# Packed attention with a feed-forward layer: where the third and fourth quarter of a batch's packs are computed

## The chip, the cores and the metric

The kernel runs on one core of a Trainium2 chip. The metric is the time of one execution on the device in microseconds. TensorE (PE in the profile) multiplies matrices, VectorE (DVE) and ScalarE (ACT) work on elements, GpSimd (POOL) adds a few weights early on, and SyncE (SP) issues the DMAs.

## The reference

For each of 8 batches and 8 heads, 32 packed queries `p` attend to 576 keys and values; the result serves as both keys and values for the 576 queries `q`. The heads are then laid side by side into 512 features, and a feed-forward layer without biases follows.

```python
def sm_attn(qq, kk, vv):
    s = scale * np.matmul(qq, kk.transpose(0, 1, 3, 2))
    s = s - np.max(s, axis=-1, keepdims=True)
    a = np.exp(s)
    a = a / (np.sum(a, axis=-1, keepdims=True) + 1e-09)
    return np.matmul(a, vv)
p_packed = sm_attn(p, k, v)                # 8 x 8 x 32 x 64
out = sm_attn(q, p_packed, p_packed)       # 8 x 8 x 576 x 64
...
x = out.transpose(0, 2, 1, 3).reshape(B * S, H * D)   # 4608 x 512
h = x @ w_in                               # 512 -> 2048
g = h * (1.0 / (1.0 + np.exp(-h)))
return g @ w_out                           # 2048 -> 512
```

All of it is float32. To keep its precision in the large products, each operand is split into an upper part (`hi`) that TensorE takes at its faster rate and the rest (`lo`), and three products hi·hi, hi·lo and lo·hi are added.

## The kernel before

**Packs.** The kernel does not form the attention's output `x`. The second attention's values are the 32 packed rows of each head, so `x @ w_in` is the attention's weights times (packed rows times the head's rows of `w_in`). This second factor is called the packs here. A batch's packs have 2048 columns and are made in four quarters of 512 (numbered 0 to 3), each by one `Packs` object: `products` (line 510) runs 16 matmuls of the 64x32 tiling through `heads` (line 250) into one buffer of the PSUM pool `ps_two`; `upper` (line 528) copies them to `pw_hi` on ScalarE; `lower` (line 531) subtracts on VectorE and gives `pw_lo`, after which the PSUM buffer is free.

**Units.** A batch's feed-forward layer is cut into 16 units, f = 0 to 15, of 128 hidden features each. A unit has a hidden block (`h_products`, line 563: 12 matmuls of 288 columns from one quarter of the packs and the second attention's weights; then `h_values`, lines 582 to 586, on ScalarE, and `h_lower`, line 593, on VectorE) and an output block (`out_products`, line 603: 12 matmuls of 512 columns). Unit f takes the quarter f // 4. The 64 tokens of a batch that don't fill a whole block of 128 are kept in `rest` and handled for two batches together, in four units of their own after every odd batch.

**Order.** The early part (batches 0 and 1, and the first steps of batch 2) follows an order written out by hand in `ORDER`. From line 761 on a loop runs over the units of batches 2 to 7. TensorE, VectorE, ScalarE and SP each execute their instructions in the order in which the program issues them; nothing is rescheduled on these four. `hidden_up_to(u + 2)` issues hidden blocks ahead, so that a unit's output block finds its values ready.

**The next batch's attention in between.** Beside the units of batch b the loop issues the attention of batch b + 1, one step at a given f (`STEPS_AT`):

- f=1, `scores1`: packed queries times keys in two halves of 288 keys, 16 matmuls each (line 250), each half into its own `ps_two` buffer; line 276 copies the first half out on ScalarE and the second on VectorE. Then the load of q and the maximum (lines 286 and 287, VectorE).
- f=2, `exps1`: exponentials on ScalarE (line 296) and the reciprocals of their sums on VectorE (lines 300 and 301).
- f=3, `turned1`: two transposes of 32x32 blocks on VectorE (line 309); then 16 small DMAs from SP (line 327), one for each pair of heads and each 32 partitions, lay the transposed blocks out over the partitions. Pair 0 is issued first, pair 3 last.
- f=7, `packed`: 80 small matmuls of these weights with v (line 348) into a `ps_two` buffer. They run over all four pairs for each chunk of keys. `scaled1` (line 358, VectorE) divides by the sums; after the unit's output block `turned` (line 367, TensorE) and `packs` (line 371, VectorE) transpose the result.
- f=9 to 12: the second attention's scores, exponentials and weights.

**PSUM.** `ps_two` has two buffers, given out in turn. Hidden blocks, quarters of packs, scores and products with v all take one each. Where a unit needs both (`all_banks`, line 772), no hidden blocks are issued ahead in it, and the next unit issues two.

**The quarters' places.** Quarters 0 and 1 of batch b + 1 are made at f = `PACKS_NEXT` = 13 of batch b. Quarters 2 and 3 are made at f = `PACKS_OWN` = 4 of the batch itself: both products, 32 matmuls in one block, then both splits. Batch 2 makes its quarters 1 and 2 earlier (line 767) and only quarter 3 at f=4. `pw_hi` and `pw_lo` have three buffers: two in `pw` and one in `pw_b`.

Of the kernel before, what the change touches and what calls it, by code (L numbers as in the profile page):

```python
# [20 lines left out]
B, H, S, D = 8, 8, 576, 64  # L21
# [9 lines left out]
FJ = JW // P  # L31
# [6 lines left out]
EARLY = 2  # L38
# [40 lines left out]
ON_POOL = (0, 1, 2, 6, 9, 10, 11, 13, 14, 15, 16, 18, 19)  # L79
ON_TOKENS = (0,)  # L80
PACKS_NEXT, PACKS_OWN = 13, 4
SCALE = 1.0 / math.sqrt(D)
EPS = 1e-9

# [4 lines left out]
def packed_attention_ffn(ctx: ExitStack, tc: tile.TileContext, pkT, qT, v, w_in, w_out, out):  # L89
# [56 lines left out]
    def load_k(b):  # L146
        t = kvq.tile([P, 5 * DM], F32, name="kvq_t")
        n = P + NI * HS
        for c in (slice(0, n), slice(n, n + NI * HS)) if b == 0 else (slice(0, P + NI * S),):
            nc.sync.dma_start(t[:, c], pkT[b, :, c])  # L150
        made["k", b] = t[:, :P], t[:, P : P + NI * S].rearrange("p (hf i s) -> p hf i s", hf=2, i=NI)

    def load_q(b):
        if b == 0:
            n = NI * MAIN
            spare = osb.tile([P, 2, DM], F32, name="o").rearrange("p r e -> p (r e)")
            parts_of_q = spare[:, :n], rest.rearrange("p f e h s -> p (f e h s)")[:, : NI * S - n]
            for t, c in zip(parts_of_q, (slice(0, n), slice(n, NI * S))):
                nc.sync.dma_start(t, qT[b, :, c])
            made["q", b] = [t.rearrange("p (i s) -> p i s", i=NI) for t in parts_of_q]  # L160
            return
        t = kvq.tile([P, 5 * DM], F32, name="kvq_t")
        nc.sync.dma_start(t[:, : NI * S], qT[b])
        t = t[:, : NI * S].rearrange("p (hf i s) -> p hf i s", hf=2, i=NI)
        made["q", b] = [t[:, 0], t[:, 1]]

    def load_v(b):
        t = kvq.tile([P, 5 * DM], F32, name="kvq_t")
        nc.sync.dma_start(t, v[b])
        made["v", b] = t.rearrange("p (c e) -> p c e", c=5)  # L170
# [84 lines left out]
    class Attention:  # L255
# [24 lines left out]
        def largest1(self, par=None):  # L280
# [5 lines left out]
            nc.vector.tensor_reduce(self.mx[:, c], s, axis=AX.X if self.b else AX.XY, op=ALU.max, negate=True)  # L286
            nc.vector.tensor_scalar(self.nm[:, c], self.mx[:, c], SCALE, None, op0=ALU.mult)

        def exps1(self, par):
# [5 lines left out]
            e = self.e1[:, par] if self.b else self.e1[:, par].rearrange("p (h s) -> p h s", h=2)  # L295
            nc.scalar.activation(e, s, AF.Exp, bias=self.nm[:, c], scale=SCALE, accum_out=self.den[:, c])  # L296

# [149 lines left out]
        def exps2(self, hf):  # L447
            if self.b in ON_TOKENS:
                _, t = self.on_tokens(hf)
                nc.scalar.activation(t, t, AF.Exp, scale=SCALE)  # L450
                return
            s2, e2 = self.half[hf]
            nc.scalar.activation(e2, s2, AF.Exp, scale=SCALE)

# [159 lines left out]
    def out_products(u, hf=None):  # L614
        b, f, *more = units[u]
        start = first_of(u)
        first = u == start
        if more:
            if first:
                acc[start, 0] = sum_banks()  # L620
            for n in range(FJ):
                products(acc[start, 0][:, 0], u, f + n, n, f + n == 0, f + n == NF - 1)
            return
        for h in range(2)[half_or_all(hf)]:
            if first:
                acc[start, h] = sum_banks()
            for k in range(2):
                products(acc[start, h][:, k], u, f, 2 * h + k, first, is_last(u))

    def out_rows(u, h):  # L630

        b, f, *more = units[u]
        sums = acc[first_of(u), h]
        if more:
            o = osb.tile([P, 2, DM], F32, name="o")
            nc.scalar.copy(o[:, 0], sums[:, 0])
            for n, (e, h) in enumerate((e, h) for e in range(2) for h in range(2)):
                at = (b + e) * S + h * HS + MAIN
                rows = slice((2 * e + h) * REST, (2 * e + h) * REST + REST)
                (nc.scalar if n % 2 and b == B - 2 else nc.sync).dma_start(out[at : at + REST], o[rows, 0])  # L640
            return
        if ("o", b, h) in outs:
            o = outs.pop(("o", b, h))
            nc.vector.tensor_tensor(o, sums, o, ALU.add)
        else:
            o = osb.tile([P, 2, DM], F32, name="o")
            (nc.vector.tensor_copy if h else nc.scalar.copy)(o, sums)
        if f == NF - 1:
            at = b * S + h * HS
            nc.sync.dma_start(out[at : at + MAIN].rearrange("(k p) e -> p k e", p=P), o)  # L650
        else:
            nc.sync.dma_start(parts[b, h], o)
# [53 lines left out]
    def hidden_up_to(u):  # L706
        nonlocal done
        while done < min(u, len(units) - 1):
            done += 1
            if len(units[done]) == 2:  # L710
                h_products(done)
            h_values(done)
            h_lower(done)

    def packs_in(b, *quarters):
        both = [Packs(b, FJ * j, FJ) for j in quarters]
        for part in both:
            part.products()
        for part in both:
            part.upper()  # L720
            part.lower()

    def step_of(b, step):
        at = attention[b]
        if step == "scores1":
            for hf in range(2):
                at.scores1(hf)
                at.copied1(hf)
            load_q(b)
            at.largest1()  # L730
        elif step == "exps1":
            for par in range(2):
                at.exps1(par)
            at.shares1()
        elif step == "turned1":
            for par in range(2):
                at.turned1(par)
            at.spread1()
        elif step == "packed":
            at.packed()  # L740
            at.scaled1()
            if b < B - 1:
                load_k(b + 1)
        elif step == "scores2":
            for hf in range(2):
                at.scores2(hf)
            for hf in range(2):
                at.turned2(hf)
            if b < B - 1:
                load_v(b + 1)  # L750
            for hf in range(2):
                at.less2(hf)
        else:
            for hf in range(2):
                if step == "split2":
                    at.upper2(hf)
                    at.lower2(hf)
                else:
                    getattr(at, step)(hf)

    for u in range(n_early, len(units)):
        b, f, *more = units[u]
        if more:
            hidden_up_to(u + 1 if u == n_early else u + 2)
            out_products(u)
            if u == n_early:
                packs_in(2, 1, 2)
            if f + FJ == NF:
                out_rows(u, 0)
            continue  # L770
        step = STEPS_AT.get(f) if b + 1 < B else None
        all_banks = step in ("scores1", "scores2") or f == PACKS_OWN or f == PACKS_NEXT and b + 1 < B
        if not all_banks:
            hidden_up_to(u + 2)
        if f == PACKS_OWN:
            packs_in(b, *((3,) if b == 2 else (2, 3)))
        if f == PACKS_NEXT and b + 1 < B:
            packs_in(b + 1, 0, 1)
        if step:
            step_of(b + 1, step)  # L780
        out_products(u)
        if f == NF - 1:
            for h in range(2):
                out_rows(u, h)
        if step == "packed":
            attention[b + 1].turned()
            attention[b + 1].packs()
# [43 lines left out]
```

## Time and profile before

| | us |
|---|---|
| Median of 3 runs | 703.89 (703.79 to 703.93) |
| The profiled execution | 703.09 |
| its span from first to last instruction | 701.3 |
| output products (line 603), three groups of 560 matmuls | 223.8 + 219.4 + 218.8 busy |
| hidden products (line 563), three groups | 154.6 + 146.5 + 145.9 busy |
| packs (line 250, from `win`), 560 matmuls | 32.8 busy |

Matmuls are pipelined, so the busy times of two groups overlap and their sum is larger than the span. The chain that ended last gives each moment to one instruction; the lengths of its pieces are used below. In its rows the columns are the start in the span, the length, the engine, the tile and line, and the number of instructions; in the timeline they are the start, the length, the engine, the line, the operation, the tiles with their shapes and the count, and in brackets how long the engine was idle before and what released it. SPq is SP's queue: its time is that of issuing a DMA, while the landing is given separately. By lines, the chain's time is distributed thus:

| line | what | share of the chain |
|---|---|---|
| 603 | output products | 58% |
| 563 | hidden products | 29% |
| 250 | packs and both attentions' scores | 7% |
| 348 | products with v | 2% |

### The profile page before, as it was taken

What the parts mean: (1) busy time and instruction counts of PE and PEld (TensorE: products, weight loads), DVE (VectorE), ACT (ScalarE), POOL (GpSimd) and SP (SyncE); (2) the same over time, 40 slices, a digit from 0 to 9 for tenths busy, and PEclk for the clock granted to TensorE, in tenths of its full rate; (3) what the DMA queues carried; (4) which work ended last, traced back from release to release, by engine and by line L of the source; (5) the groups of instructions that cost most, each with busy time, mean ns of one, the idle gap of its engine ahead of it and who ended that gap; (6) DMA issues with size and microseconds to landing.
All of it is one profiled execution on the core that took longest, in us unless ns stands there. A gap on an engine that the chain in (4) does not pass through costs nothing.

```text
span 701.3 us, 12059 instructions
## 1 busy us (share of the span) xinstructions
PE 693.3 (99%) x5058; PEld 560.5 (80%) x5058; DVE 326.2 (47%) x482; ACT 331.0 (47%) x614; POOL 28.7 (4%) x19
## 2 busy tenths in 40 slices
PE   8999999999999999999999999999999999999997
PEld 5557788878787888888788888878878788788886
DVE  4999948764534136333532335342372323622111
ACT  4997866637245244451633526452442533433221
POOL 1041022110000000000000000000000000000000
PEclk9999999999999999999999999999999999999999
DMA  9775333634221320313012131123202120010002
GB/s 358 288 304 206 134 121 114 193 141 156 70 81 69 77 104 1 128 33 137 12 61 84 27 107 49 61 72 70 110 0 76 68 36 1 1 60 1 1 1 75
DMA packets 28309, 64.61 MB, mean 92 GB/s; under 512 B 16736, under 2 KB 16736, under 8 KB 23904
## 3 DMA queue, kind: packets, MB, share of 16 engines
q1 hardware_dynamic: 28160, 63.71, 26.2%
q8 instruction: 40, 0.66, 0.4%
q10 hardware_dynamic: 96, 0.13, 0.1%
q14 instruction: 13, 0.11, 0.0%
HBM read 48.76 MB, written 11.53 MB: 86 GB/s over the span
## 4 chain that ended last, share of the span: by engine, by line
PE 97%; ACT 1%; DMA 1%; DVE 1%; issue 0%; ACTq 0%; DVEq 0%
PE ps_acc L603 58%; PE ps_two L563 29%; PE ps_two L250 7%; PE ps_two L348 2%; DMA kvq_t<-in_pkT 1%; PE ps_acc L250 0%; ACT tm L296 0%; PE ps_two L144 0%; ACT tm L392 0%; ACT w_raw L201 0%; ACT win L201 0%; PE ps_two L315 0%; PE ps_two L367 0%; PE ps_acc L315 0%; DVE mx L286 0%
## 5 line engine op out<-in xcount | busy, mean ns | idle before, releaser
L603 PE MATMUL ps_acc<-wo_hi,g_hi 128*128 128x512 f32 x560 | 223.8, 400 | 0.0
L603 PE MATMUL ps_acc<-wo_hi,g_lo 128*128 128x512 f32 x560 | 219.4, 392 | 0.0
L603 PE MATMUL ps_acc<-wo_lo,g_hi 128*128 128x512 f32 x560 | 218.8, 391 | 0.0
L593 DVE TENSOR_TENSOR g_lo<-g,g_hi 128x512 fp32r<-128x512 f32 x124 | 88.9, 717 | 259.5 <-ACT g_hi L584 259.5
L582 ACT ACTIVATE g<-ps_two 128x512 f32<-128x512 f32 x124 | 74.1, 598 | 263.9 <-PE ps_two L563 239.9
L563 PE MATMUL ps_two<-a_lo,pw_hi 128*128 128x288 f32 (+2 forms) x528 | 154.6, 301 | 0.1
L563 PE MATMUL ps_two<-a_hi,pw_hi 128*128 128x288 f32 (+1 forms) x496 | 146.5, 295 | 0.0
L563 PE MATMUL ps_two<-a_hi,pw_lo 128*128 128x288 f32 (+1 forms) x496 | 145.9, 294 | 0.0
L603 PEld LDWEIGHTS ps_acc<-wo_hi,g_hi 128*128 128x128 f32 x560 | 105.1, 188 | 39.3 <-issue 19.9
L603 PEld LDWEIGHTS ps_acc<-wo_hi,g_lo 128*128 128x128 f32 x560 | 105.1, 188 | 24.5 <-DVE g_lo L593 0.4
L603 PEld LDWEIGHTS ps_acc<-wo_lo,g_hi 128*128 128x128 f32 x560 | 105.2, 188 | 18.4
L563 PEld LDWEIGHTS ps_two<-a_lo,pw_hi 128*128 128x128 f32 x528 | 99.1, 188 | 6.2 <-issue 1.4
L563 PEld LDWEIGHTS ps_two<-a_hi,pw_hi 128*128 128x128 f32 x496 | 93.1, 188 | 4.5 <-issue 0.8
L563 PEld LDWEIGHTS ps_two<-a_hi,pw_lo 128*128 128x128 f32 x496 | 93.2, 188 | 0.0
L584 ACT ACTIVATE g_hi<-ps_two 128x512 fp32r<-128x512 f32 x124 | 73.6, 593 | 10.9 <-PE ps_acc L603 10.9
L531 DVE TENSOR_TENSOR pw_lo<-ps_two,pw_hi 128x1024 fp32r<-128x1024 f32 x31 | 36.8, 1219 | 12.8 <-ACT pw_hi L528 12.8
L528 ACT CAST pw_hi<-ps_two 128x1024 fp32r<-128x1024 f32 x31 | 30.2, 1015 | 20.9 <-PE ps_two L250 20.9
L250 PE MATMUL ps_two<-win,ppT 64*32 64x512 f32 (+1 forms) x560 | 32.8, 560 | 0.4 <-POOL win L220 0.4
L586 ACT ACTIVATE rest<-ps_two 128x64 f32<-128x64 f32 x112 | 25.9, 231 | 0.0
L582 ACT ACT_TABLE_LOAD x16 | 20.5, 1283 | 1.5 <-PE ps_two L563 1.0
L250 PEld LDWEIGHTS ps_two<-win,ppT 64*32 64x32 f32 x560 | 7.9, 105 | 14.5 <-issue 11.1
L573 ACT CAST g_hi<-rest 128x512 fp32r<-128x512 f32 x16 | 9.9, 624 | 13.5 <-PE ps_acc L603 13.2
(122 smaller groups left out, 485.0 us busy)
## 6 DMA issues: line engine op xcount, KB each, us to landing
kvq_t<-in_v SPq DMA_DIRECT2D x8, 1280.0 KB, 6.1
kvq_t<-in_pkT SPq DMA_DIRECT2D x7, 1216.0 KB, 6.6
out<-o SPq DMA_DIRECT2D x16, 512.0 KB, 2.8
kvq_t<-in_qT SPq DMA_DIRECT2D x7, 1152.0 KB, 6.5
w_raw<-in_w_in SPq DMA_DIRECT2D x6, 1024.0 KB, 7.5
win<-in_w_out SPq DMA_DIRECT2D x3, 1024.0 KB, 4.5
w_raw<-in_w_out SPq DMA_DIRECT2D x3, 1024.0 KB, 6.2
parts<-o SPq DMA_DIRECT2D x4, 512.0 KB, 5.0
```

Of the source, the lines that this page charges most:

```text
L250: nc.tensor.matmul(bank(par)[NP * i : NP * i + NP], lhs(r, i), rhs(r, i), start=True, stop=True)
L348: nc.tensor.matmul(self.ps[NP * i : NP * i + NP, par * D : par * D + D], e, vs[:n, c, h * D : h * D + D], start=(c == 0), stop=(c == 4),)
L528: nc.scalar.copy(self.hi, self.ps[:, :, : self.nf * P])
L531: nc.vector.tensor_tensor(self.lo, self.ps[:, :, : self.nf * P], self.hi.bitcast(F32), ALU.subtract)
L563: nc.tensor.matmul(bank, p[:, par, cols], a[:, par], start=(n == 0), stop=(n == len(todo) - 1))
L573: nc.scalar.copy(g_hi, g)
L582: nc.scalar.activation(g, ps[..., :MAIN], AF.Silu)
L584: nc.scalar.activation(g_hi, ps[..., :MAIN], AF.Silu)
L586: nc.scalar.activation(to, ps[..., MAIN:HS], AF.Silu)
L593: nc.vector.tensor_tensor(g_lo[:, c], g[:, c], g_hi[:, c].bitcast(F32), ALU.subtract)
L603: nc.tensor.matmul(bank, g[:, rows], w[:, at], start=(first and n == 0), stop=(last and n + 1 == len(todo)))
```

## The change

Quarters 2 and 3 lose their block at f=4, except in batch 7, which has no next batch. Quarter 2 is now made in the step `scores1` of the next batch (f=1): its products stand between the products of the scores' two halves, its splits behind the second half's copy and ahead of the load of q and the maximum. Quarter 3 is made in the step `packed` (f=7): its products right behind the 80 products with v, its splits behind `scaled1` and ahead of the load of the keys after next. In batch 2 only quarter 3 moves, since its quarter 2 is made early as before. Because `all_banks` now holds at f=7 and no longer at f=4, the hidden block that was issued at f=7 comes at f=8, together with that unit's own, and f=4 issues one where f=5 issued two.

```diff
+BETWEEN = {"scores1": 2, "packed": 3}
...
-    def step_of(b, step):
+    def step_of(b, step, between):
         at = attention[b]
         if step == "scores1":
             for hf in range(2):
                 at.scores1(hf)
                 at.copied1(hf)
+                if hf == 0 and between:
+                    between.products()
+            if between:
+                between.upper()
+                between.lower()
             load_q(b)
             at.largest1()
...
         elif step == "packed":
             at.packed()
+            between.products()
             at.scaled1()
+            between.upper()
+            between.lower()
             if b < B - 1:
                 load_k(b + 1)
...
         step = STEPS_AT.get(f) if b + 1 < B else None
-        all_banks = step in ("scores1", "scores2") or f == PACKS_OWN or f == PACKS_NEXT and b + 1 < B
+        own = BETWEEN.get(step)
+        between = Packs(b, FJ * own, FJ) if own and (b > EARLY or own == 3) else None
+        alone = {PACKS_OWN: (b, 2, 3)} if b == B - 1 else {PACKS_NEXT: (b + 1, 0, 1)}
+        all_banks = between or step in ("scores1", "scores2") or f in alone
         if not all_banks:
             hidden_up_to(u + 2)
-        if f == PACKS_OWN:
-            packs_in(b, *((3,) if b == 2 else (2, 3)))
-        if f == PACKS_NEXT and b + 1 < B:
-            packs_in(b + 1, 0, 1)
+        if f in alone:
+            packs_in(*alone[f])
         if step:
-            step_of(b + 1, step)
+            step_of(b + 1, step, between)
         out_products(u)
```

## Prediction

> **What bounds the kernel now.** I read the page first: the busy shares, the granted clock by slices, and the shares of the chain that ended last.
>
> ```profile
> PE 693.3 (99%) x5058; PEld 560.5 (80%) x5058; DVE 326.2 (47%) x482; ACT 331.0 (47%) x614; POOL 28.7 (4%) x19
> ...
> PEclk9999999999999999999999999999999999999999
> ...
> PE 97%; ACT 1%; DMA 1%; DVE 1%; issue 0%; ACTq 0%; DVEq 0%
> ```
>
> TensorE is busy 99% of the span at a granted clock that never leaves the top, and the chain is TensorE's for 97%. So any microsecond taken from TensorE's own stream is won, and any wait put into it is lost whole. VectorE and ScalarE, at 47%, matter only where TensorE waits for them. Next I read the chain in order of time around one change site, batch 4 with batch 5's attention in it (start, length, line, count):
>
> ```profile
> 388.40 2.77 PE ps_acc L603 x12
> 391.17 1.88 PE ps_two L250 x32
> 393.05 2.94 PE ps_acc L603 x12
> 395.99 3.16 PE ps_two L563 x24
> 399.15 2.77 PE ps_acc L603 x12
> 401.92 1.58 PE ps_two L563 x12
> 403.49 2.77 PE ps_acc L603 x12
> 406.26 1.58 PE ps_two L563 x12
> 407.84 1.66 PE ps_two L348 x80
> ```
>
> In the code's terms: output products of f=3; the block of two quarters (f=4); output products of f=4; two hidden blocks; f=5; one hidden block; f=6; one hidden block; the products with v (f=7). Nothing stands between the pieces. An output block takes 2.77, but 2.94 behind the quarters' block, so leaving that 64*32 tiling costs 0.17. A hidden block is 1.58.
>
> **What the products with v wait for.** Their weights are the tile that 16 small DMAs of line 327 spread; these wait for two VectorE transposes (line 309), issued one after the other from SP. The timelines of VectorE and SP, and the line's own view with its landings:
>
> ```profile
> 391.60 1.43 DVE L309 STREAM_TRANSPOSE tm<-tm 128x576 f32<-128x576 f32 x2
> ...
> 226.59 10.28 SPq L327 DMA_DIRECT2D tm<-tm  x16
> 303.96 11.24 SPq L327 DMA_DIRECT2D tm<-tm  x16
> 393.09 11.37 SPq L327 DMA_DIRECT2D tm<-tm  x16
> 471.30 11.44 SPq L327 DMA_DIRECT2D tm<-tm  x16
> 560.43 10.84 SPq L327 DMA_DIRECT2D tm<-tm  x16
> ...
> L327 SPq DMA_DIRECT2D tm<-tm x16: 594/602/1681, 393.1 to 403.9; - x16
> ...
> L327 SPq DMA_DIRECT2D tm<-tm x2: 601/602/602, 403.2 to 403.9; - x2
> DMA to landing us min/median/max: 1.9/1.9/1.9
> ```
>
> The transposes end at 393.03, and SP starts at 393.09. It issues for 10.3 to 11.4 us; the last DMA takes 0.60 to issue and lands 1.9 after its issue began, so a batch's last landing is SP start + length + 1.3. In the shown batch: 393.09 + 11.37 + 1.3 = 405.76, against products with v at 407.84: about 2.1 us to spare. No row of the page shows it, because nothing waits there today.
>
> **The change part by part.** TensorE's own work first. The single-quarter block of batch 2, and the place before the loops where products with v already have a quarter right behind them, in the same chain:
>
> ```profile
> 144.20 1.70 PE ps_two L348 x76
> ...
> 145.96 0.86 PE ps_two L250 x12
> ...
> 224.67 1.02 PE ps_two L250 x16
> 225.69 2.96 PE ps_acc L603 x12
> ```
>
> *Removed* at f=4: in batches 3 to 6, 1.88 + 0.17 = 2.05; in batch 2, 1.02 + 0.19 (2.96 against 2.77) = 1.21. *Added*: a quarter inside a block that is already in this tiling costs 1.88 − 1.02 = 0.86, for the third between the scores' halves. The fourth behind the products with v: from 144.20 to 145.96 + 0.86 = 146.82 both took 2.62, and alone they take 1.66, so 0.96. Batches 3 to 6 save 2.05 − 0.86 − 0.96 = 0.23 each, batch 2 saves 1.21 − 0.96 = 0.25: **1.17 us** in all. Batch 7 keeps its block, and no instruction is added or lost.
>
> The Trainium skill (TensorEngine Tiling (Array Packing), Key Properties) says that changing the tiling mode, not just the tile, drains TensorE. By it the step from 128*32 to 64*32 behind the products with v is a drain too, and moving the fourth quarter there trades one drain for another; at 0.17 for a drain that quarter would cost 1.03 instead of 0.96, and the saving would be 0.82 instead of 1.17. The rows agree that a switch costs, but show only 0.10 for this one, and I keep the row.
>
> *Moved.* Two things leave the stretch between the transposes and the products with v: the block at f=4, and the hidden block of f=7, since a unit with a quarter in it now skips the hidden blocks (they come as a pair at f=8). The transposes do not move against the f=3 products: scores, exponentials and f=3 shift together by the quarter added ahead of them. The 16 issues on SP are not moved either, and have nothing new ahead of them. So the products with v come 1.88 + 0.17 + 1.58 = 3.63 us earlier against their DMAs (batch 2: 1.02 + 0.19 + 1.58 = 2.79). The other four sites in the chain:
>
> ```profile
> 240.50 1.66 PE ps_two L348 x80
> ...
> 318.69 1.66 PE ps_two L348 x80
> ...
> 486.03 1.66 PE ps_two L348 x80
> ...
> 575.18 1.66 PE ps_two L348 x80
> ```
>
> On the old clock, arrival against last landing: 237.71 against 226.59 + 10.28 + 1.3 = 238.17, wait 0.46; 315.06 against 316.50, 1.44; 404.21 against 405.76, 1.55; 482.40 against 484.04, 1.64; 571.55 against 572.57, 1.02. Sum **6.11 us**. The first round of products goes through all four pairs of heads, and the last pair's weights are those issued last, so only three of 80 matmuls could run ahead. What is queued behind the wait on TensorE is everything: the quarter, the f=7 output products, the next hidden blocks. Nothing else can fill it.
>
> *Restart after a wait.* No TensorE wait of this kind is in the trace. Below nothing is possible by about 0.1, as the tiling switch at the entry then lies in the wait; above, the line's semaphore instructions bound it: 45 in five sites, so 9 × 0.051 = 0.46 if all came after the landing.
>
> ```profile
> L348 PEldq EVENT_SEMAPHORE  x45: 51/51/51, 237.4 to 573.6; - x45
> ```
>
> Most of the nine will have been met before, as most of the DMAs have landed; I take 0.1 each, **0.5 us**. The SP lengths differ by one long issue (1.68 in the shown batch, where the median is 0.60). At the first site's 10.28 everywhere, 0.96 + 1.09 + 1.16 + 0.56 = 3.8 us of the waits would go; I keep them, since SP's instructions stay the same, and keep the loss for the range.
>
> *The scores' second half* now reuses the first half's bank and waits for ScalarE's copy of it; the third quarter's 0.86 is its cover. The chain's and both engines' rows:
>
> ```profile
> 376.82 1.13 PE ps_two L250 x32
> 377.95 2.94 PE ps_acc L603 x12
> ...
> 377.57 0.64 ACT L276 COPY tm<-ps_two 128x576 f32<-128x576 f32 x1 [2.28 <-PE ps_two L250]
> ...
> 378.06 0.76 DVE L276 COPY tm<-ps_two 128x576 f32<-128x576 f32 x1 [2.16 <-PE ps_two L250]
> 378.93 1.35 DVE L286 TENSOR_REDUCE mx<-tm 128x2 f32<-128x1152 f32 x1
> ...
> 383.63 0.69 DVE L593 TENSOR_TENSOR g_lo<-g,g_hi 128x512 fp32r<-128x512 f32 x1 [3.15 <-ACT g_hi L584]
> ...
> 392.30 1.93 ACT L528 CAST pw_hi<-ps_two 128x1024 fp32r<-128x1024 f32 x2 [1.22 <-PE ps_two L250]
> ...
> 393.34 2.36 DVE L531 TENSOR_TENSOR pw_lo<-ps_two,pw_hi 128x1024 fp32r<-128x1024 f32 x2 [0.31 <-ACT pw_hi L528]
> ```
>
> A signal takes 0.11 (block end 377.95, copy 378.06), so the first half ended near 377.46, the quarter would end at 378.32, and the copy's end is seen at 378.21 + 0.11 = 378.32. A dead heat; ends 0 and 0.64 (no cover). I take 0.05 in four batches, **0.2 us**. Behind it, upper (0.97) and lower (1.18) free the quarter's bank some 2.6 us after its products, with VectorE's own copy (0.76) ahead; the next hidden block comes 0.48 + 2.94 = 3.4 later, so 0.8 stays. Behind the products with v the same pair needs about 2.4 and has 2.95: hidden as well. If this cover went, each bank would cost TensorE what is missing.
>
> **Sum**: −1.17 + 6.11 + 0.5 + 0.2 = +5.6 us. The profiled execution took 703.09 (span 701.3 and 1.8 around it), so 708.7 there; the median is 703.89, 0.8 above it, so **709.5**.
>
> **The rivals.** *The spread is in time* (not slower): the last landing comes before f=6's output products end, which decides at 1.0 to 1.6 us in four batches. Then only the saving stays: 703.89 − 1.17 = 702.7. For it: 2.1 us to spare today, and the long issues might go. Against it: 3.63 us are taken away, and even 16 issues of 0.60 with their landing fill most of the rest.
>
> *The copy is late*: if ScalarE's copy is not covered, 4 × 0.59 more, 711.9. Against it: ScalarE was idle 2.28 before it.
>
> *The maximum is late*: the third quarter's lower (1.18) stands ahead of the reduction on VectorE; were the exponentials late by it, the transposes and so the waits would grow by 4 × 1.18, to 714.2. Against it: with the quarter's 0.86 ahead the reduction would end at 378.93 + 0.86 + 1.18 + 1.35 = 382.3, and VectorE's next work, shifted alike, comes at 384.5.
>
> *The clock drops.* TensorE's longest wait in the view of waits is 1.4, with the clock at the top throughout:
>
> ```profile
> PE ps_two L144 <- POOL ident masks.py:199: 1.4, 1, 1.4
> ```
>
> Three of the new waits are longer. If each halved the clock over the next output block (2.95), 709.5 + 8.9 = 718.4. The Trainium skill (TensorE: Matmul & The Clock Gate, What's actually happening) has the clock halved after at least one idle window of about 3.4 us, and by that rule none of these waits, at most 1.64, would do it; no run here shows a wait long enough to test it.
>
> **How the numbers follow.** Forecast, waits for the spread: 0.81. Spread in time: 0.09. Copy late: 0.04. Maximum late: 0.03. Clock: 0.03. Within the forecast the waits' sum moves most: without the long issues +1.9 remains; with all semaphores behind the landing +7.4, and with longer issues more. The range 706.0 to 712.5 covers most of the forecast and the late copy, and leaves out the spread in time, the clock, the late maximum and the forecast's low tail, under 0.2. A measurement tells about 0.2%, 1.4 us, from no change. Slower 0.87; same 0.09 (most of the spread in time, with a tail of the forecast); faster 0.04 (a saving slightly above 1.17).
>
> **What would show it.** In the changed profile: TensorE idle ahead of line 348's weight loads, released by the DMA of line 327, five times, smallest in the first; SP's 16 issues as long as before; no block at f=4; some 0.96 of line 250 behind the products with v; TensorE's other pieces as long as before. The forecast is wrong if SP's last issue starts over a microsecond earlier against the f=3 products, or if the waits stand at the scores instead.

## The result, and the profile after

| | us |
|---|---|
| before, median of 5 | 703.79 (703.72 to 703.93) |
| changed, median of 5 | 709.53 (708.24 to 711.75) |
| ratio, 95% interval | 1.0083 (1.0064 to 1.0102) |
| profiled execution of the changed kernel, its span | 708.24, 706.5 |

The change costs 5.7 us. It also spreads the times: over five runs each, 0.2 us lie between the fastest and the slowest before and 3.5 us after (beside the experiments, over more runs, the kernel before spread by 1.6 to 2.0). The profiled execution is the fastest of the five, so the sizes read from it are at the low end. Line numbers of the changed kernel are one higher than before.

The page of the changed kernel: busy shares, the chain's shares by engine and by line, and the group of the products with v, which has an idle time and a releaser that were not there before.

```profile
PE 694.0 (98%) x5058; PEld 560.2 (79%) x5058; DVE 326.4 (46%) x482; ACT 331.4 (47%) x614; POOL 28.7 (4%) x19
...
PE 83%; SPq 6%; ACT 4%; DMA 3%; DVE 2%; issue 1%; POOL 0%; ACTq 0%
PE ps_acc L604 50%; PE ps_two L564 24%; PE ps_two L251 7%; SPq L328 5%; DMA w_raw<-in_w_in 2%; PE ps_two L349 2%; DMA tm<-tm 1%; ACT g L583 1%; ACT g_hi L585 1%; DVE tm L310 1%; ACT L583 1%; ACT L297 1%; ACT tm L297 1%; DVE g_lo L594 1%; POOL win L221 0%
...
L349 PE MATMUL ps_two<-kvq_t,tm 128*32 128x64 f32 (+1 forms) x560 | 13.9, 224 | 4.3 <-DMA tm<-tm 4.0
```

The busy share tells little: TensorE fell from 99% to 98%. The chain tells it: TensorE's part fell from 97% to 83%, and SP's queue at line 328, the issue of the spread DMAs, is on it with 5%. Where TensorE waits, the chain leaves it and goes back through what made it wait. The same stretch of batch 4 as before, in the chain of the changed kernel (start, length, what):

```profile
378.89 2.16 PE ps_two L251 x48
381.06 2.94 PE ps_acc L604 x12
384.00 1.59 PE ps_two L564 x12
...
391.68 1.28 ACT L583
394.70 1.44 DVE tm L310 x2
...
398.78 1.75 SPq L328
...
407.04 1.88 DMA tm<-tm
409.05 1.63 PE ps_two L349 x70
410.74 0.86 PE ps_two L251 x12
411.60 2.95 PE ps_acc L604 x12
```

Read upward: the products with v were released by a DMA's landing, that by SP's issues (one of them 1.75 long), those by VectorE's transposes, and ahead of those stand the exponentials and a unit's hidden values on ScalarE. The other side, in the timelines of TensorE and of SP:

```profile
407.24 0.31 PE L349 MATMUL ps_two<-kvq_t,tm 128*32 128x64 f32 x6
409.05 1.63 PE L349 MATMUL ps_two<-kvq_t,tm 128*32 128x64 f32 x70 [1.50 <-DMA tm<-tm]
...
305.65 11.16 SPq L328 DMA_DIRECT2D tm<-tm  x16
396.20 11.44 SPq L328 DMA_DIRECT2D tm<-tm  x16
476.01 10.27 SPq L328 DMA_DIRECT2D tm<-tm  x16
```

Six matmuls run, then TensorE idles 1.50 us. By the prediction's rule the last landing is at 396.20 + 11.44 + 1.3 = 408.94; the matmuls go on at 409.05. At the other four sites TensorE idles 0.32, 1.24, 0.38 and 0.84 us.

### The profile page after: what moved, and what is told of

It is laid out like the page before. It is cut to its first block, busy times and chain, and to the rows that moved or that the text cites. A ratio compares the mean times of both kernels' runs of the same rounds, so it can differ in the third digit from the quotient of the medians.

```text
span 706.5 us, 12060 instructions
## 1 busy us (share of the span) xinstructions
PE 694.0 (98%) x5058; PEld 560.2 (79%) x5058; DVE 326.4 (46%) x482; ACT 331.4 (47%) x614; POOL 28.7 (4%) x19
## 2 busy tenths in 40 slices
DMA packets 28309, 64.61 MB, mean 91 GB/s; under 512 B 16736, under 2 KB 16736, under 8 KB 23904
## 4 chain that ended last, share of the span: by engine, by line
PE 83%; SPq 6%; ACT 4%; DMA 3%; DVE 2%; issue 1%; POOL 0%; ACTq 0%
PE ps_acc L604 50%; PE ps_two L564 24%; PE ps_two L251 7%; SPq L328 5%; DMA w_raw<-in_w_in 2%; PE ps_two L349 2%; DMA tm<-tm 1%; ACT g L583 1%; ACT g_hi L585 1%; DVE tm L310 1%; ACT L583 1%; ACT L297 1%; ACT tm L297 1%; DVE g_lo L594 1%; POOL win L221 0%
## 5 line engine op out<-in xcount | busy, mean ns | idle before, releaser
L349 PE MATMUL ps_two<-kvq_t,tm 128*32 128x64 f32 (+1 forms) x560 | 13.9, 224 | 4.3 <-DMA tm<-tm 4.0
L349 PEld LDWEIGHTS ps_two<-kvq_t,tm 128*32 128x32 f32 (+1 forms) x560 | 10.0, 108 | 9.9 <-issue 6.7
```

The source lines that it names most:

```text
L349: nc.tensor.matmul(self.ps[NP * i : NP * i + NP, par * D : par * D + D], e, vs[:n, c, h * D : h * D + D], start=(c == 0), stop=(c == 4),)
```

## The experiments

The theory: the loss is the wait for the spread DMAs, because the quarters' block and one hidden block no longer lie ahead of the products with v; the scores' second half adds a small wait for the copy. The rivals: the third quarter between the scores delays what follows there; the fourth quarter's new place costs by itself; putting the hidden block off costs by itself.

| run | median | ratio to before, 95% interval |
|---|---|---|
| third quarter only | 704.93 | 1.0014 (1.0005 to 1.0023) |
| fourth quarter only | 705.34 | 1.0022 (1.0012 to 1.0033) |
| changed, hidden block ahead | 703.12 | 0.9993 (0.9984 to 1.0001) |
| the same, first copy split | 704.67 | 1.0013 (1.0004 to 1.0022) |
| changed, two queues | 702.50 | 0.9981 (0.9972 to 0.9989) |
| before, hidden block put off | 704.04 | 1.0007 (0.9998 to 1.0016) |
| hidden block ahead and two queues | 702.28 | 0.9981 (0.9972 to 0.9990) |
| before, two queues | 703.48 | 0.9992 (0.9983 to 1.0001) |

The kernel before ran beside each: 703.75 for the first four, 703.61 for the next three, 703.99 for the last. The changed kernel did not run beside them; where a run is compared with it, its 709.53 is that of the result.

**Third quarter only.**

```diff
-BETWEEN = {"scores1": 2, "packed": 3}
+BETWEEN = {"scores1": 2}
...
             at.packed()
-            between.products()
             at.scaled1()
-            between.upper()
-            between.lower()
...
-        alone = {PACKS_OWN: (b, 2, 3)} if b == B - 1 else {PACKS_NEXT: (b + 1, 0, 1)}
+        alone = {PACKS_OWN: (b, 2, 3)} if b == B - 1 else {PACKS_OWN: (b, 3), PACKS_NEXT: (b + 1, 0, 1)}
```

> Only the third quarter is moved between the scores' halves; the fourth keeps a block of its own at f=4, and the hidden block stays at f=7. Theory (the loss is the wait for the spread DMAs, since 3.63 us of cover were taken away; the scores' second half waits 0.18 each time for the copy): the cover shrinks by only 0.84 of the 2.0 to 2.6 us to spare, so no wait at line 348's products; TensorE pays 1.21 + 0.86 instead of 2.05, and 4 x 0.18 at the scores: 703.8 + 0.8 = 704.6. Rival (the third quarter between the scores delays the maximum and the exponentials, and that is the loss): most of the 5.7 us stays, 707 or more.

1.2 us slower than before; 0.8 was expected, which the interval (0.0005 to 0.0023 of 703.75, so 0.4 to 1.6) holds, and 3 or more would have been the rival's. No TensorE row of the profile at the products with v waits for a DMA; at the scores the block is long, and the fourth quarter stands alone later. In the chain:

```profile
377.75 2.17 PE ps_two L251 x48
...
393.13 1.02 PE ps_two L251 x16
```

Without a wait the 48 matmuls would take 1.13 + 0.86 = 1.99. So each of four scores' blocks pays 0.18, or 0.7 in all, and that is the only price of this half that was found; the other 0.5 lies within the interval. The delay of the maximum is refuted as the cause.

**Fourth quarter only.**

```diff
-BETWEEN = {"scores1": 2, "packed": 3}
+BETWEEN = {"packed": 3}
...
-        between = Packs(b, FJ * own, FJ) if own and (b > EARLY or own == 3) else None
+        between = Packs(b, FJ * own, FJ) if own else None
         alone = {PACKS_OWN: (b, 2, 3)} if b == B - 1 else {PACKS_NEXT: (b + 1, 0, 1)}
+        if EARLY < b < B - 1:
+            alone[PACKS_OWN] = (b, 2)
```

> Only the fourth quarter is moved behind the products with v; the third keeps a block of its own at f=4. Theory: the cover shrinks by 0.84 + 1.58 = 2.42 us (batch 2: 2.79), against 2.0 to 2.6 to spare, so waits of 0.2 to 0.5 us remain in most batches, 1.4 in all and 0.1 each for the restart; the blocks cost 0.2 more than before: 703.8 + 2.1 = 705.9, between 704.5 and 707.5. Rival (the quarter behind the products with v costs about 1 us each by itself, whatever the cover): 708 to 709.

1.6 us slower, inside the expected bounds. The profiled execution is the slowest of the eight (707.35); 2.4 us of it are lost at an early place that the edit does not touch, which is shown under the control below. At the five sites the stretch from the last matmul of f=6's output products to the first of f=7's is 1.0, 0.4 and 0.3 us longer in the first three than in the last two, which run through. The first, second and fourth:

```profile
241.39 1.63 PE L349 MATMUL ps_two<-kvq_t,tm 128*32 128x64 f32 x70 [0.75 <-DMA tm<-tm]
...
320.04 1.63 PE L349 MATMUL ps_two<-kvq_t,tm 128*32 128x64 f32 x70 [0.17 <-DMA tm<-tm]
...
487.72 1.67 PE L349 MATMUL ps_two<-kvq_t,tm 128*32 128x64 f32 x76
```

The two halves together would make 1.2 + 1.6 = 2.8 us, half of the change's 5.7. That is the mark of a slack used up by both: either half alone takes less than what was to spare, or little more, and the rest of what both take is paid whole.

**The changed kernel with the hidden block ahead.**

```diff
-        all_banks = between or step in ("scores1", "scores2") or f in alone
+        all_banks = step in ("scores1", "scores2") or f in alone
```

> The changed kernel, but with the hidden block issued at f=7 ahead of the products with v, as before the change. Theory: 1.58 us of cover come back, and the waits of 0.5 to 1.65 shrink to at most 0.2 each; what is left is the saving of 1.17 against 0.72 at the scores: 703.4, between 703.0 and 704.2. Rival (the fourth quarter's place is itself the loss): 708 or more.

703.12. One hidden block put back ahead of the products with v removes 6.4 us against the changed kernel, though both quarters stay in their new places. The chain at the same site, and at one of the two where a remnant is left:

```profile
317.88 1.83 PE ps_two L349 x76
...
405.53 1.58 PE ps_two L564 x12
407.11 1.60 PE ps_two L349 x76
408.77 0.86 PE ps_two L251 x12
409.63 2.96 PE ps_acc L604 x12
```

From 407.11 to 409.63 the products with v and the quarter take 2.52 where nothing waits. At 317.88 the same products take 0.23 longer, and two batches later 0.15. Against the kernel before, the interval reaches 1.0001, so this version alone is not shown to be faster.

**The same with the first half's copy split over two engines.** This edit comes on top of the last one.

```diff
+            if hf == 0 and self.b > EARLY + 1:
+                nc.scalar.copy(self.s1[:, 0, :HS], self.s1_banks[:, 0, :HS])
+                nc.vector.tensor_copy(self.s1[:, 1, :HS], self.s1_banks[:, 1, :HS])
+                return
```

> As the run with the hidden block ahead, and the copy of the scores' first half is split: one bank on ScalarE, the other on VectorE, in place of both on ScalarE. Theory: each copy takes about 0.35 to 0.4 instead of 0.64, the bank is free before the third quarter's products end, and the 0.18 in each of four batches goes: 0.7 less than that run, 702.7, below the kernel before by 1.1. Rival (the 0.18 is a drain or a weight load at the change of tiles and no wait for the copy): as that run, 703.4.

Slower by 1.5 us than without the split: a miss, but one that decides between the two readings. The timeline at one scores' block:

```profile
377.85 0.40 ACT L278 COPY tm<-ps_two 128x288 f32<-128x288 f32 x1 [2.28 <-PE ps_two L251]
378.27 0.46 DVE L279 COPY tm<-ps_two 128x288 f32<-128x288 f32 x1 [2.10 <-ACT tm L278]
...
378.79 0.18 PEld L251 LDWEIGHTS ps_two<-kvq_t 64*32 64x32 f32 x16 [1.10 <-DVE tm L279]
```

The two copies did not run side by side: VectorE's began when ScalarE's ended, and the profile names it as the releaser. One after the other they take 0.88 instead of 0.64, and the second half of the scores comes later by the difference. That makes 1.0 of the 1.5 in four batches; the rest was not traced. So what is waited for there is the copy, not a drain. Both copies read one PSUM tile and write one tile in SBUF. In the kernel before, two copies into that SBUF tile overlap (ScalarE's from 377.57 to 378.21, VectorE's from 378.06), but they read two PSUM tiles; so the order seems to come from the one PSUM tile. No run tests that.

**The changed kernel with two queues.**

```diff
-                        nc.sync.dma_start(self.e1T[NP * at : NP * at + NP, : some.shape[1], i], some)
+                        (nc.gpsimd if at % 2 else nc.sync).dma_start(self.e1T[NP * at : NP * at + NP, : some.shape[1], i], some)
```

> The changed kernel as it is, but every second one of the 16 spread DMAs is issued from GpSimd's queue, which is idle then, instead of SP's. Theory (SP's serial issue of 16 DMAs at 0.65 us is what the products with v wait for): SP issues eight in 5.2 us, GpSimd's eight run beside them, the last landing comes some 4 us earlier than TensorE, and all five waits go: 702.8, between 702.4 and 704. Rival (the time is the transfers' or the landing's, whoever issues): 708 to 710.

702.50: 7.0 us less than the changed kernel, with TensorE's order untouched. The timelines of SP and of GpSimd, and the chain:

```profile
393.93 6.24 SPq L328 DMA_DIRECT2D tm<-tm  x8
...
394.52 4.52 POOL L328 DMA_DIRECT2D tm<-tm  x8 [84.47 <-DVE tm L310]
...
402.27 2.77 PE ps_acc L604 x12
405.04 1.60 PE ps_two L349 x76
...
406.70 0.86 PE ps_two L251 x12
407.56 2.95 PE ps_acc L604 x12
```

SP has issued by 400.17, GpSimd by 399.04, and the products with v start at 405.04 without a wait, right behind the output products. The bytes are the same (64.61 MB in the whole run), though GpSimd's half travels in 1536 packets where SP used 7680 for it. A spread DMA takes as long from issue to landing as before (median 2.1 against 2.0), so it is the serial issue on one queue that the changed kernel waits for, and not the transfers.

**The kernel before with the hidden block put off.**

```diff
-        all_banks = step in ("scores1", "scores2") or f == PACKS_OWN or f == PACKS_NEXT and b + 1 < B
+        all_banks = step in ("scores1", "packed", "scores2") or f == PACKS_OWN or f == PACKS_NEXT and b + 1 < B
```

> The kernel before, with its block of two quarters at f=4, but the hidden block of f=7 is issued at f=8, behind the products with v, as in the changed kernel. Theory: 1.58 us of cover go out of 2.0 to 2.6 to spare, so no wait, and the time stays: 703.8, at most 704.5 where SP has a second long issue. Rival (putting the hidden block off costs TensorE by itself, for instance by a pair of hidden blocks at f=8): five times some 0.5 us or more, 706.

704.04 against 703.61, with 1 inside the interval: putting the block off costs nothing that can be measured while the quarters' block is still there. It is close, though. In the chain and SP's timeline of this run:

```profile
404.14 2.77 PE ps_acc L603 x12
406.90 1.66 PE ps_two L348 x80
...
393.74 11.60 SPq L327 DMA_DIRECT2D tm<-tm  x16
```

The last landing is at 393.74 + 11.60 + 1.3 = 406.64, and TensorE came at 406.90: 0.3 us to spare.

**Both cures, and the control.** Both runs take the edit of the two queues; one adds it to the version with the hidden block ahead, the other to the kernel before.

> The hidden block ahead of the products with v, and the spread DMAs on the two queues: the waits of 0.23 and 0.15 that two batches still had go as well. Theory: 702.7, below the kernel before by about 1. Rival (nothing was left to gain, or GpSimd's queue costs something elsewhere): 703.1 or more.

> The kernel before, with the spread DMAs on the two queues and nothing else changed. Theory: they had 2.0 to 2.6 us to spare already, so an earlier landing gains nothing and the 1.1 us of the changed kernel with two queues are the change's own: 703.7, within 0.3 of the kernel before. Rival (the queues bring the gain, not the quarters' places): 702.6.

702.28, 1.3 us below the kernel before, and within the noise of the run with two queues alone. The control came to 703.48 against 703.99, where at most 0.3 was expected; its interval holds no change, and a gain of up to 1.2 us too.

The traces show one place where two queues help without the change: the early products with v near 144 us, which no edit touches. The v that they need is loaded from SP right behind the 16 spread DMAs, so a long issue holds it up. SP's timeline and the chain, for the kernel before, for the run with only the fourth quarter moved, and for the control:

```profile
137.10 0.53 SPq L169 DMA_DIRECT2D kvq_t<-in_v  x1
144.20 1.70 PE ps_two L348 x76
...
140.44 0.54 SPq L170 DMA_DIRECT2D kvq_t<-in_v  x1
146.38 2.25 PE ps_two L349 x76
...
132.96 0.54 SPq L169 DMA_DIRECT2D kvq_t<-in_v  x1
144.84 1.60 PE ps_two L348 x76
```

This v lands 6.4, 5.7 and 6.0 us after its issue began, so at 143.5, 146.1 and 139.0. The products take 1.60 in all three runs with two queues, 1.70 in the kernel before, and 2.05 to 2.25 in the six other runs with one; in the second pair of rows TensorE also idles 1.77 before them. That the load of v is the cause is read from these times; no row names it as the releaser.

So two queues gain some tenths there by themselves. The changed places of the quarters gain 1.67 − 0.72 = 0.95 by the sizes worked out below, once the DMAs come in time; the runs (1.1 with two queues and the change, 0.5 with two queues alone) differ by 0.6, which agrees with that within their noise and does not settle it further. Either changed version with two queues beats both kernels.

## Why the prediction was right

The cause is the one named, and the time came out at 709.53 against 709.5. That the two agree so closely is luck: five runs spread by 3.5, and the errors cancel in part. The sum was +5.6, where the two profiled executions differ by 5.15; and 0.8 was added for the way from the profiled execution to the median, where it is 1.3 after the change.

- **What bounds it** held: TensorE's other pieces are as long as before (2.77, 1.58, 2.94), and a wait in its stream is lost whole.
- **The wait for the spread** is shown by three runs: more cover removes it, an earlier landing removes it, and either half of the change alone uses up little more than the slack. Its size was 6.1 + 0.5 for restarts. In the profiled execution the stretch from the end of f=6's output products to the start of f=7's is 3.10, 4.00, 4.27, 3.15 and 3.61 us, against 2.52 without a wait: 5.5 in all. Most of the difference is one site: SP took 10.27 at 476.01, without the long issue that made it 11.44 in the execution that the sum was made from. The restart was sized right: in the shown stretch 0.11 from landing to matmul. Six matmuls, not three, ran ahead of the wait, since each of the 40 products in the code is two matmuls in the trace; that changed little.
- **The saving** was mis-sized: 1.17 was forecast. The quarter behind the products with v costs 2.52 − 1.66 = 0.86, not the 0.96 read from the place ahead of the loops, where the products themselves ran longer (1.70 instead of 1.60, the late v of the control's section). The 0.10 that the prediction read as the price of a change of tiling is that difference. There is no such change at the quarter: the last chunk of keys has 64 rows, so the last products with v run in the 64*32 tiling already, as in the changed kernel's timeline:

```profile
410.47 0.63 PE L251 MATMUL ps_two<-win,ppT 64*32 64x512 f32 x4
410.50 0.24 PE L349 MATMUL ps_two<-kvq_t,tm 64*32 64x64 f32 x4
```

With 0.86 the saving is 4 × 0.33 + 0.35 = 1.67.

- **The scores' second half** was called a dead heat at 0.05; it costs 0.18 in each of four batches, 0.7 in all. These rows of the changed kernel's timeline show it:

```profile
289.09 0.64 ACT L277 COPY tm<-ps_two 128x576 f32<-128x576 f32 x1 [2.28 <-PE ps_two L251]
...
289.78 0.18 PEld L251 LDWEIGHTS ps_two<-kvq_t 64*32 64x32 f32 x16 [0.85 <-ACT tm L277]
```

The copy ends at 289.73 and the weights are loaded at once, but not before. I had compared the copy's end with the end of the quarter's products, and left out that the weights of the second half, loaded ahead otherwise, wait too.

- The sum by these sizes: −1.67 + 5.53 + 0.72 = +4.6, against 708.24 − 703.09 = 5.15 between the two profiled executions. Of the 0.6 left, 0.43 lies ahead of the first changed instruction: the single-quarter block that begins at 188.48 before begins at 188.91 after. Most of that is the early products with v (2.06 after, 1.70 before).
- **The late maximum** did not happen: the transposes start 3.2 us after the f=3 output products begin, before (388.40 to 391.60) and after (384.00 + 3.16 + 2.77 + 1.58 = 391.51 to 394.70).
- **The clock** did not drop. The stretches around the longest wait (stretch, length, then busy time and count of TensorE, its weight loads, VectorE, ScalarE and GpSimd, clock, DMA share, GB/s):

```profile
406.00:409.50 3.50, 2.00 (x38) 1.38 (x36) 0.39 (x1) 0.00 (x0) 0.00 (x0) 1.00 0.25 42
409.50:416.00 6.50, 6.50 (x98) 4.84 (x90) 1.81 (x3) 1.01 (x1) 0.00 (x0) 1.00 0.53 194
```

The clock stays at 1.00 through 1.50 us of idle and after it. The Trainium skill (TensorE: Matmul & The Clock Gate, What's actually happening) has it halved after at least one idle window of about 3.4 us. The wait shown is shorter and the clock held, which agrees; TensorE's longest wait in any of these runs is 1.77, so the rule itself is not tested.

The wider spread of the times is explained only by argument: SP's long issues vary between executions, and now they lie on the path at five more places. At the early place they lay on it already: the execution of 707.35, with only the fourth quarter moved, had 15.19 us of issues there, the others with one queue 11.98 to 13.05. There is one trace for each kernel, so this was not followed run by run.

## What to carry to other kernels

Before work is moved on the engine that bounds a kernel, look at what it covers and not only at what it costs: here 3.63 us of useful work stood between a transfer's start and its use, and no row of the waits said how little was to spare. Compute the slack of each producer that the moved stretch hides (landing against use, per site), and compare it with what is taken away. Where many small DMAs are issued from one queue, their serial issue is the length to shorten; a second idle queue removed all five waits here and left TensorE's order as it was, while the hidden block put back ahead left two remnants. What is queued behind such a series is late with it, as the early v was.

## What was not expected of the hardware

- Sixteen spread DMAs take SP 10.3 us at the least, 0.65 each, and in most batches one of them takes 0.9 to 1.9. GpSimd issued eight in 4.5 us, 0.57 each, beside SP.
- The quarter behind the products with v costs 0.86, as inside a block of its own tiling. The last of these products run in 64*32 too, so no change of tiling lies ahead of it. Leaving 64*32 for 128*128 costs 0.17. The Trainium skill (TensorEngine Tiling (Array Packing), Key Properties) has every change of mode drain TensorE. The 0.17 agrees with that; what a change from 128*32 to 64*32 costs was not worked out here.
